# Diagonal score groups as ten blocks of sixteen in a gated attention and maxout kernel on one Trainium2 core

## The chip, the cores and the metric

The kernel runs on one core of a Trainium2 chip. The core has a matrix engine (TensorE, PE in the profile, with its weight loads listed as PEld), three engines for elementwise work (VectorE or DVE, ScalarE or ACT, GpSimd or POOL), a queue engine that only issues transfers here (SyncE or SP), and 16 DMA engines. Data are computed in SBUF, a memory of 128 partitions. TensorE writes to PSUM, from which VectorE and ScalarE fetch its results. The engines run side by side, each through its own instructions in order, and semaphores tie them together. The metric is the device time of one execution in microseconds.

## The reference

```python
scores = scale * np.matmul(z, z.transpose(0, 2, 1))   # z: 8 x 3072 x 64, scale = 1/3072
attn = np.maximum(scores, 0.0) ** 2
x = (u * np.matmul(attn, v)).reshape(24576, 256)      # u, v: 8 x 3072 x 256
h1, h2 = x @ w1, x @ w2                               # w1, w2: 256 x 1024
out = np.maximum(h1, h2) @ w_out                      # w_out: 1024 x 256
```

The scores of a sequence are a product of z with itself, so the matrix of 3072 by 3072 scores is symmetric. There is no softmax: ReLU and square act on each element.

## The kernel before

**Tiling.** A sequence (there are eight) is 24 blocks of 128 rows. Four blocks make a group (`G = 4`), so there are six groups and six steps per sequence, 48 steps in all. Step `n` with group `s` produces the output rows of group `s`; it needs the 512 columns of scores of that group against all six groups of keys. Because the scores are symmetric, a group of scores above the diagonal is computed once and turned by a DMA transpose for the step that needs its mirror image (`add_pair`, job `turn`, tiles `a_sb` to `aT`). The first three steps of the first sequence work without turned tiles.

**The diagonal group** of a step is 4 by 4 blocks of 128 by 128, itself symmetric. `add_diag` (L384) does it in 45 of the 48 steps. Before the change it computes 12 of the 16 blocks: rows 0 and 1 in full, as two matmuls of 512 columns into a PSUM tile of two banks (`scores`), and the lower right quarter of rows 2 and 3 as matmuls of 256 columns into another tile (`scores_low`). The upper right quarter, four blocks, is turned into the lower left one by one DMA transpose within `a_sb` (`do_turn`). The group is stored in `a_sb` as four quarters one behind the other; `blocks` (L488) names the quarters `R(k, t)` for the readers.

**Pairs and the shared tile.** 44 of the 45 diagonal groups come in pairs of neighbouring steps (`st.pair` is 0 or 1; step 3 is alone). A pair shares one PSUM tile, key -1, for its lower right quarters: bank 0 holds those of the first group, bank 1 those of the second. A ReLU (`relu_low`) and a square of half the width of the other ones belong to each group's part.

**Half rows.** A score has 64 terms, so `score` (L209) takes partitions 0 to 63 for one matmul and 64 to 127 for the next (`half`), and the two use the two halves of the array, each into a PSUM bank of its own.

**Sums and products.** Each group of 2 by 2 half-groups is multiplied with v by a scheme of seven products instead of eight. VectorE forms the sums S1 to S4 of quarters (`add_sums`; for diagonal groups S1 is written in place over `R(1, 1)`), and TensorE does the products in two passes: `X` with three products, straight from the quarters, and `Y` with four, from the sums. Behind that come the multiplication with u and the two dense layers (`add_second`: jobs `d`, `g`, `o`, `oc`), three steps late. The second dense layer uses max(h1, h2) = max(h1 - h2, 0) + h2.

**PSUM.** Score tiles, tiles of the dense layers and the shared tiles take turns on three PSUM buffers (`mm_psum`), in the order in which TensorE fills them. A tile can be begun when the one three places ahead of it has been read out.

**The order of work.** The order of TensorE's jobs is written out: the products of all steps in a row (`work`), with visits of up to three score tiles (`windows`) put between them so many nanoseconds ahead of their readers (`laid`). A paired diagonal visit is the three tiles `(n, None)`, `(n, -1)` and `(n + 1, None)` (L1018). For all other engines a planner runs at build time: each job has a cost per engine (`RELU`, `SQUARE`, `TT` and their half-width forms, `PE` costs, SP's cost of a turn), a lag until its result can be used, and a due time that follows from TensorE's plan. The planner simulates the engines with these numbers, picks the next job of each, and decides for ReLUs, squares and copies whether ScalarE or VectorE does them (`left_to_act`, L1374). The program is issued in that order. Turns and stores are issued by SP, loads of u, v, z and weights by POOL.

Of the kernel before, what the change touches and what calls it, by code (L numbers as in the profile page):

```python
# [11 lines left out]
def kernel(  # L12
# [27 lines left out]
    P = 128  # L40
    NSB = S // P
    G = 4
    WIN = 3
    GW = G * P
# [34 lines left out]
    def matmul(*args, **kw):  # L79
        newest[0] = pin(nc.tensor.matmul(*args, **kw)).ins  # L80

    def sp_dma(**kw):
        pin(nc.sync.dma_start(**kw))
# [57 lines left out]
    q = seqs[0]  # L141
# [33 lines left out]
    def job(key, ways, fn, deps=(), new=None, uses=(), after=(), lag=100):  # L175
        assert key not in jobs, key
        jobs[key] = Job(key, ways, fn, deps, new, uses, after, lag)

    def buf(pool, key, make):
        bufs[pool, key] = Buf(make)  # L180
        order.setdefault(pool, []).append(key)

    def tile_of(pool, key):
        return bufs[pool, key].tile
# [24 lines left out]
    def score(q, out_ps, j, k, s, q0, n):  # L209
        half = ds(j * dqk, dqk)  # L210
        matmul(
            out_ps,
            q.zT[half, k + 1 - j, :],
            q.zT[half, ds(G * s + 1 - j + q0, n), :],
            start=True,
            stop=True,
        )

    def turn(out_ap, in_ap):
        sp_dma(out=out_ap, in_=in_ap, transpose=True)  # L220

    def relu(eng, out_ap, in_ap):
        if eng == "ACT":
            pin(nc.scalar.activation(out_ap, in_ap, AF.Relu))  # L224
        else:
            pin(nc.vector.tensor_single_scalar(out=out_ap, in_=in_ap, scalar=0.0, op=ALU.max))  # L226

    def square(eng, ap):
        if eng == "ACT":
            pin(nc.scalar.activation(ap, ap, AF.Square))  # L230
        else:
            pin(nc.vector.tensor_mul(ap, ap, ap))  # L232
# [20 lines left out]
    PE256, PE512, SWITCH = 109, 216, 100  # L253
    TT = {256: 205, 512: 336, 1024: 603}
    RELU = {"ACT": 912, "DVE": 1140}
    RELU_HALF = {"ACT": 480, "DVE": 610}
    SQUARE = {"ACT": 955, "DVE": 603}
    SQUARE_HALF = {"ACT": 530, "DVE": 336}
    COPY_O = {"ACT": 470, "DVE": 610}
    PATIENCE = 200  # L260
    TURN, TURN_LAG, UT_LAG = 1750, 4000, 7000
# [2 lines left out]
    def a_key(n, g):  # L264
        return ("T", ("held", n, g)) if n < HELD and g > 3 else ("A", (n, g))

    def a_tile(st, g):
        return tile_of(*a_key(st.n, g))
# [52 lines left out]
    def s_tile(key):  # L321
        return tile_of("mm", key)
# [4 lines left out]
    def add_pair(st, k0, head=None):  # L327
# [33 lines left out]
        if g > st.s and not direct(st.b, st.s, g):  # L361
# [19 lines left out]
                lag=TURN_LAG + (5000 if st.plain else 0),  # L381
            )

    def add_diag(st):  # L384
        n, q, g = st.n, st.q, st.s
        k = G * g
        a = ("A", (n, g))
        buf("A", (n, g), lambda: apool.tile([P, G, GW], bf16, name="a_sb"))

        def halves():
            return a_tile(st, g).rearrange("p r c -> p (r c)").rearrange("p (h r c) -> p h r c", h=2, r=G)

        def low_blocks():
            return halves()[:, 1, 2:4, :]

        def scores(_):
            for j in range(2):
                score(q, s_tile((n, None))[:, j, :], j, k + j, g, 0, G)  # L400

        low = ("mm", (n - (st.pair or 0), -1))

        def scores_low(_):

            ps = tile_of(*low)
            for r in range(2):
                if st.pair is None:
                    score(q, ps[:, r, : 2 * P], r, k + 2 + r, g, 2, 2)
                else:  # L410
                    for i in range(2):
                        score(q, ps[:, i, ts(r, 2 * P)], i, k + G * i + 2 + r, g + i, 2, 2)

        job(("score", n, None), {"PE": 223}, scores, deps=z_deps(st), new=("mm", (n, None)), lag=150)
        if st.pair != 1:
            job(
                ("score", n, -1),
                {"PE": 112 if st.pair is None else 223},
                scores_low,
                deps=z_deps(st),  # L420
                new=low,
                lag=150,
            )

        def relu_low(eng):
            ps = tile_of(*low)
            if st.pair is None:
                relu(eng, low_blocks(), ps[:, :, : 2 * P])
            else:
                relu(eng, low_blocks(), ps[:, st.pair, :].rearrange("p (r c) -> p r c", r=2))  # L430

        job(
            ("relu", n, None),
            RELU,
            lambda eng: relu(
                eng, halves()[:, :, 0:2, :], s_tile((n, None)).rearrange("p r (h c) -> p h r c", h=2)
            ),
            deps=[("score", n, None)],
            new=a,
            uses=[("mm", (n, None)), a],  # L440
            lag=200,
        )
        job(
            ("relu", n, -1),
            RELU_HALF,
            relu_low,
            deps=[("score",) + low[1]],
            uses=[low, a],
            after=[("relu", n, None)],
            lag=200,  # L450
        )
        job(
            ("square", n, None),
            SQUARE,
            lambda eng: square(eng, halves()[:, :, 0:2, :]),
            deps=[("relu", n, None)],
            uses=[a],
            lag=200,
        )
        job(  # L460
            ("square", n, -1),
            SQUARE_HALF,
            lambda eng: square(eng, low_blocks()),
            deps=[("relu", n, -1)],
            uses=[a],
            lag=200,
        )
        def do_turn(_):
            turn(
                halves()[:, 0, 2:4, :].rearrange("p r (q x) -> p (r q) x", x=P),  # L470
                halves()[:, 1, 0:2, :].rearrange("p r c -> p (r c)"),
            )

        job(
            ("turn", n, None),
            {"SP": 900},
            do_turn,
            deps=[("square", n, None)],
            uses=[a],
            lag=4500,  # L480
        )


# [4 lines left out]
    def blocks(st, g, k, t):  # L488
        if g in st.early:
            turned = tile_of("T", (st.b, g, st.s))  # L490
            return turned.rearrange("p (t j) (k m) x -> p t k j m x", t=2, k=2)[:, t, k]
        if st.diag and g == st.s:
            part = a_tile(st, g).rearrange("p r c -> p (r c)")[:, ts(2 * t + k, GW)]
            form = "p (j m x) -> p m j x" if (k, t) == (1, 0) else "p (m j x) -> p m j x"
            return part.rearrange(form, j=2, m=2)
        return a_tile(st, g).rearrange("p (k m) (t x) -> p k t m x", k=2, t=2)[:, k, t]

    def sums(st, g, f):
# [514 lines left out]
    windows, room = [], 0  # L1013
    for i, (n, k0) in enumerate(tiles):
        if k0 is None and steps[n].pair == 1:
            continue
        if k0 == -1 and steps[n].pair == 0:
            windows.insert(len(windows) - (room > 0), [(n, None), (n, -1), (n + 1, None)])  # L1018
        elif k0 is not None or steps[n].pair is None:
            if not room or (k0 is None and room < 2):  # L1020
                windows.append([])
                room = 2 if n == 0 else WIN
            windows[-1].append((n, k0))
            room -= 1
        if tiles[i + 1 : i + 2] and tiles[i + 1][0] // NG > n // NG:
            room = 0

    begins, t = [], 0
# [19 lines left out]
    for n in range(PLAIN, len(steps)):  # L1048
        i = first_of[n]
# [13 lines left out]
    for w in reversed(range(len(windows))):  # L1063
        limit = min([limit] + [due[r] for r in windows[w] if r in due])
        found = [i for i in spots if begins[i] <= limit]
        i = found[-1] if found else 0
# [26 lines left out]
    def at_step(b, s, us):  # L1093
        return pe_job_at(starts[NG * b + s] + us * 1000)

    def z_deps(st):
        return [("zT", st.b)] if st.b else []
# [45 lines left out]
    for n in range(len(steps)):  # L1143
        b, s = steps[n].b, steps[n].s
        if n == 0:
            add_u(0, None)
        else:
            pb, ps = divmod(n - 1, NG)
# [15 lines left out]
    for tile_sb, source, key, at, new, rows in (  # L1164
# [20 lines left out]
        lag=3500,  # L1185
# [10 lines left out]
    def w2o_products(_):  # L1196
# [18 lines left out]
        lag=150,  # L1215
    )
    for dc in range(KD):
# [6 lines left out]
            lag=200,  # L1224
# [6 lines left out]
    for args in plain_todo:  # L1231
        st, i, ks, dcs = args
# [28 lines left out]
    def held(key):  # L1261
        return a_key(key[1], key[2] // G)[0] == "T"

    slots = sorted(
        [
            (position[at_step(0, key[1] + 2, 1)[0]] if held(key) else position.get(key, -1), k)
            for key, k in turned_order
        ]
        + [(position.get(key, -1), ("held", key[1], k[2])) for key, k in turned_order if held(key)]
        + [(position[at_step(0, 0, 7)[0]], "w2"), (position[at_step(0, 1, 7)[0]], "w2T")],  # L1270
        key=lambda x: x[0],
    )
# [18 lines left out]
    for pool, keys in order.items():  # L1291
        for i, k in enumerate(keys):
            j = taker.get((pool, k))
# [20 lines left out]
    plan, t = {}, 0  # L1314
    for key, before in zip(pe_order, [None] + pe_order):
        j = jobs[key]
# [4 lines left out]
    count = {j.key: len(j.succ) for j in jobs.values()}  # L1321
    stack = [j for j in jobs.values() if not j.succ]
    seen = 0
    while stack:
        j = stack.pop()
# [53 lines left out]
    while len(emitted) < len(jobs) - len(HEAD):  # L1379
        best = None  # L1380
        for e, todo in ready.items():
# [5 lines left out]
            at, _, j = min(found, key=lambda x: x[:2])  # L1387

            late_ones = [x for x in found if x[0] <= at + PATIENCE and x[1] < min(at, j.due)]
            if e != "PE" and late_ones:  # L1390
                at, _, j = min(late_ones, key=lambda x: x[1])
# [3 lines left out]
        at, e, j = best  # L1395
# [93 lines left out]
```

## Time and profile before

| what | value |
|---|---|
| median of three runs | 926.64 us (926.61 to 926.68) |
| the profiled execution's own time | 926.78 us |
| its span | 925.0 us |
| granted TensorE clock | 1.0 of full |
| VectorE busy | 786.2 us, 85% |
| ScalarE busy | 658.3 us, 71% |
| share of q1 (transposes, stores) and q0 (loads) of the 16 DMA engines | 66.9% and 22.6% |
| score matmuls of 512 and of 256 columns | 594 and 90 |
| turns within `a_sb`, and from `a_sb` to `aT` | 45 and 230 |

How to read the profile: the page gives the busy time of each engine, the span in 40 slices, and the chain of work that ended last, followed back from the end. A group of instructions has its line, engine and operation, what it writes and reads (`s_ps<-zT`), the sizes, the number of instructions, then busy time, the mean length of one, and idle time ahead. All matmuls are issued by one helper and so have line 80; they are told apart by their tiles. The timeline lists instructions in order of time, and merges equal ones that follow each other (x8 is eight of them, with the length from the first's start to the last's end); where shapes differ, the first one's is shown. Matmuls are pipelined: a matmul of 512 columns has a recorded length of 379 ns, but the next one starts 216 ns later. So starts are compared, not lengths.

### The profile page before, as it was taken

To read this page: it belongs to the slowest core of one execution; us is meant where nothing else is said; L and a number is where in the kernel's file an instruction comes from. 1 tells how busy PE (TensorE), PEld (TensorE's weight loads), DVE (VectorE), ACT (ScalarE), POOL (GpSimd) and SP (SyncE) were. 2 spreads that over 40 slices of the span, in tenths; PEclk is the share of its full clock that TensorE was granted. 3 is DMA by queue.
4 is the path that set the end of the run, shared out by engine and by line. 5 is a ranking of instruction groups with operands and counts; after the bars stand their busy time and mean duration, and the time that the engine had idled before them with its cause. 6 is when DMAs were issued, how large, how long until landed. Compare 5 with 4: busy or idle time off the path is not lost.

```text
span 925.0 us, 18991 instructions
## 1 busy us (share of the span) xinstructions
PE 918.9 (99%) x7339; PEld 669.8 (72%) x7343; DVE 786.2 (85%) x1955; ACT 658.3 (71%) x785; POOL 58.4 (6%) x115
## 2 busy tenths in 40 slices
PE   8999999999999999999999999999999999999998
PEld 3367777777767776787767877778777786777786
DVE  7948999788998889988899888998789977999661
ACT  8867968758686677856788477884878839787334
POOL 2100100000000000000000010001000010000000
PEclk9999999999999999999999999999999999999999
DMA  9999999988999989999999879999899997997611
GB/s 157 163 197 180 179 184 166 156 152 142 175 169 144 155 145 183 153 148 151 152 185 165 148 131 176 167 164 150 150 151 178 158 168 129 175 151 137 127 35 69
DMA packets 371339, 142.55 MB, mean 154 GB/s; under 512 B 349744, under 2 KB 351408, under 8 KB 371248
## 3 DMA queue, kind: packets, MB, share of 16 engines
q1 hardware_dynamic: 354688, 111.59, 66.9%
q0 software_dynamic: 16560, 29.74, 22.6%
q8 instruction: 57, 0.93, 0.4%
q14 instruction: 34, 0.28, 0.1%
HBM read 59.77 MB, written 25.17 MB: 92 GB/s over the span
## 4 chain that ended last, share of the span: by engine, by line
PE 99%; DMA 0%; ACT 0%; issue 0%; DVE 0%
PE s_ps L80 50%; PE acc L80 49%; DMA o_sb<-in_z_dram 0%; ACT a_sb L230 0%; ACT a_sb L224 0%; PE tpz L109 0%; DVE zT L110 0%; ACT o_sb L235 0%; DVE z_sb L154 0%
## 5 line engine op out<-in xcount | busy, mean ns | idle before, releaser
L80 PEld LDWEIGHTS <-v_sb 128*128 128x128 bf16 x2304 | 224.0, 98 | 79.5 <-issue 37.4
L224 ACT ACTIVATE a_sb<-s_ps 128x1024 bf16<-128x1024 f32 x211 | 204.1, 1019 | 42.3 <-PE s_ps L80 40.8
L80 PE MATMUL acc<-es,v_sb 128*128 128x256 bf16 x864 | 195.8, 274 | 0.0
L80 PE MATMUL s_ps<-w_out_sb,g_sb 128*128 128x256 bf16 x1504 | 194.9, 273 | 0.0
L230 ACT ACTIVATE a_sb<-a_sb 128x1024 bf16<-128x1024 bf16 (+1 forms) x201 | 192.4, 999 | 0.1
L224 ACT ACTIVATE g_sb<-s_ps 128x1024 bf16<-128x1024 f32 x188 | 177.3, 1030 | 11.0 <-PE s_ps L80 10.9
L80 PEld LDWEIGHTS <-lf 128*128 128x128 bf16 x1620 | 158.5, 98 | 22.2
L80 PE MATMUL s_ps<-xT,w_sb 128*128 128x512 bf16 x768 | 173.4, 379 | 0.0
L80 PE MATMUL acc<-es,lf 128*128 128x256 bf16 x756 | 170.8, 273 | 0.0
L80 PE MATMUL acc<-a_sb,lf 128*128 128x256 bf16 x612 | 166.9, 273 | 0.0
L80 PEld LDWEIGHTS <-g_sb 128*128 128x128 bf16 x1504 | 147.1, 98 | 17.3
L80 PE MATMUL acc<-aT,v_sb 128*128 128x256 bf16 x684 | 146.7, 273 | 0.0
L80 PE MATMUL acc<-a_sb,v_sb 128*128 128x256 bf16 (+1 forms) x737 | 143.3, 291 | 0.6 <-issue 0.3
L238 DVE TENSOR_TENSOR es<-a_sb 128x512 bf16<-128x512 bf16 x306 | 122.3, 416 | 25.3 <-PE acc L80 25.0
L235 ACT COPY e<-acc 128x512 f32<-128x512 f32 x90 | 53.0, 589 | 114.9 <-PE acc L80 114.9
L80 PEld LDWEIGHTS <-w_sb 128*128 128x128 bf16 x768 | 75.1, 98 | 80.8
L226 DVE TENSOR_SCALAR a_sb<-s_ps 128x1024 bf16<-128x1024 f32 (+1 forms) x127 | 129.9, 1032 | 1.3 <-PE s_ps L80 0.7
L235 ACT COPY o_sb<-s_ps 128x512 f32<-128x512 f32 (+1 forms) x84 | 48.3, 575 | 91.1 <-PE s_ps L80 91.0
L238 DVE TENSOR_TENSOR es<-aT 128x512 bf16<-128x512 bf16 x126 | 51.2, 418 | 48.0 <-PE acc L80 48.0
L80 PE MATMUL s_ps<-zT 64*128 64x512 bf16 (+1 forms) x684 | 89.7, 366 | 0.3 <-DVE zT L110 0.3
L232 DVE TENSOR_TENSOR a_sb<-a_sb 128x1024 bf16<-128x1024 bf16 (+1 forms) x137 | 86.6, 653 | 0.1
L80 PE MATMUL s_ps<-W2o_sb,xT 128*128 128x256 bf16 x384 | 73.3, 273 | 0.0
(59 smaller groups left out, 726.4 us busy)
## 6 DMA issues: line engine op xcount, KB each, us to landing
out_dram<-o_sb SPq DMA_DIRECT2D x47, 512.0 KB, 4.1
v_sb<-in_v_dram POOLq DMA_DIRECT2D x48, 256.0 KB, 5.2
u_sb<-in_u_dram POOLq DMA_DIRECT2D x48, 256.0 KB, 5.5
aT<-a_sb SPq DMA_TRANSPOSE x230, 4.5
z_sb<-in_z_dram POOLq DMA_DIRECT2D x7, 384.0 KB, 6.2
w_sb<-in_moe_w_dram POOLq DMA_DIRECT2D x2, 512.0 KB, 6.7
uT<-u_sb SPq DMA_TRANSPOSE x48, 4.3
a_sb<-a_sb SPq DMA_TRANSPOSE x45, 2.6
```

The lines of the kernel that those rows point to most:

```text
L80: newest[0] = pin(nc.tensor.matmul(*args, **kw)).ins
L224: pin(nc.scalar.activation(out_ap, in_ap, AF.Relu))
L226: pin(nc.vector.tensor_single_scalar(out=out_ap, in_=in_ap, scalar=0.0, op=ALU.max))
L230: pin(nc.scalar.activation(ap, ap, AF.Square))
L232: pin(nc.vector.tensor_mul(ap, ap, ap))
L235: pin(nc.scalar.copy(out_ap, in_ap) if eng == "ACT" else nc.vector.tensor_copy(out_ap, in_ap))
L238: pin(nc.vector.tensor_add(*args))
```

## The change

A diagonal group is computed as ten of its sixteen blocks, and `a_sb` holds it as 16 slots of one block each.

- The group's own PSUM tile holds eight blocks: (0,0), (0,1), (0,2), (0,3), (2,2), (2,3), (1,2) and (1,3), by four matmuls of 256 columns (two on each half of the array) instead of two of 512. The ReLU puts them into slots 0 to 7 in an order that has the six blocks above the diagonal in slots 2 to 7.
- The shared tile holds the remaining two blocks of each group, (1,1) and (3,3): four matmuls of 128 columns for a pair instead of four of 256, and a ReLU and a square of 256 elements instead of 512 for each group. They go to slots 14 and 15.
- The DMA turns six blocks, slots 2 to 7 into slots 8 to 13, instead of four.
- Readers find a quarter by a first slot, a row step and a column step (`DIAG_SLOTS`, `diag_blocks`) instead of as a contiguous piece.
- The planner's costs follow: 264 and 345 ns for the shared ReLU instead of 480 and 610, 318 and 205 for its square instead of 530 and 336, 60 ns of TensorE for one group's last blocks, 1300 for SP's turn instead of 900, 4700 for its lag instead of 4500.
- In a paired visit the shared tile is the last of the three instead of the middle one.

```diff
-    RELU_HALF = {"ACT": 480, "DVE": 610}
+    RELU_LAST = {"ACT": 264, "DVE": 345}
-    SQUARE_HALF = {"ACT": 530, "DVE": 336}
+    SQUARE_LAST = {"ACT": 318, "DVE": 205}
+    LAST_BLOCKS = 60
...
+    DIAG_SLOTS = {(0, 0): (0, 10, 4), (0, 1): (2, 1, 4), (1, 0): (8, 4, 1), (1, 1): (1, 10, 4)}
+
+    def diag_slots(a):
+        return a.rearrange("p r (s x) -> p (r s) x", x=P)
+
+    def diag_blocks(a, first, row, col):
+        start = diag_slots(a)[:, first, :]
+        return bass.AP(
+            tensor=start.tensor,
+            offset=start.offset,
+            ap=[list(start.ap[0]), [row * P, 2], [col * P, 2], [1, P]],
+        )
...
         def scores(_):
-            for j in range(2):
-                score(q, s_tile((n, None))[:, j, :], j, k + j, g, 0, G)
+            for i in range(2):
+                for j, (row, col) in enumerate(((0, 0), (0, 2)) if i == 0 else ((2, 2), (1, 2))):
+                    score(q, s_tile((n, None))[:, j, ts(i, 2 * P)], j, k + row, g, col, 2)
...
             for r in range(2):
+                row = 2 * r + 1
                 if st.pair is None:
-                    score(q, ps[:, r, : 2 * P], r, k + 2 + r, g, 2, 2)
+                    score(q, ps[:, r, :P], r, k + row, g, row, 1)
                 else:
                     for i in range(2):
-                        score(q, ps[:, i, ts(r, 2 * P)], i, k + G * i + 2 + r, g + i, 2, 2)
+                        score(q, ps[:, i, ts(r, P)], i, k + G * i + row, g + i, row, 1)
...
-                {"PE": 112 if st.pair is None else 223},
+                {"PE": LAST_BLOCKS if st.pair is None else 2 * LAST_BLOCKS},
...
-                relu(eng, low_blocks(), ps[:, :, : 2 * P])
+                relu(eng, slots(14, 2), ps[:, :, :P])
             else:
-                relu(eng, low_blocks(), ps[:, st.pair, :].rearrange("p (r c) -> p r c", r=2))
+                relu(eng, slots(14, 2), ps[:, st.pair, : 2 * P].rearrange("p (r x) -> p r x", r=2))
...
-                eng, halves()[:, :, 0:2, :], s_tile((n, None)).rearrange("p r (h c) -> p h r c", h=2)
+                eng,
+                slots(0, 8).rearrange("p (j r) x -> p j r x", j=2),
+                s_tile((n, None)).rearrange("p h (r j x) -> p j (h r) x", r=2, j=2),
...
-            lambda eng: square(eng, halves()[:, :, 0:2, :]),
+            lambda eng: square(eng, slots(0, 8)),
...
-            lambda eng: square(eng, low_blocks()),
+            lambda eng: square(eng, slots(14, 2)),
...
-            turn(
-                halves()[:, 0, 2:4, :].rearrange("p r (q x) -> p (r q) x", x=P),
-                halves()[:, 1, 0:2, :].rearrange("p r c -> p (r c)"),
-            )
+            turn(slots(8, 6), slots(2, 6).rearrange("p s x -> p (s x)"))
...
-            {"SP": 900},
+            {"SP": 1300},
...
-            lag=4500,
+            lag=4700,
...
-            part = a_tile(st, g).rearrange("p r c -> p (r c)")[:, ts(2 * t + k, GW)]
-            form = "p (j m x) -> p m j x" if (k, t) == (1, 0) else "p (m j x) -> p m j x"
-            return part.rearrange(form, j=2, m=2)
+            return diag_blocks(a_tile(st, g), *DIAG_SLOTS[k, t])
...
-            windows.insert(len(windows) - (room > 0), [(n, None), (n, -1), (n + 1, None)])
+            windows.insert(len(windows) - (room > 0), [(n, None), (n + 1, None), (n, -1)])
```

More of the change, by code (lines that the diff above doesn't have):

```diff
@@ L388, in add_diag, with slots @@
         buf("A", (n, g), lambda: apool.tile([P, G, GW], bf16, name="a_sb"))
[L392 to L396, printed above, removed]
+        def slots(first, count):
+            return diag_slots(a_tile(st, g))[:, ds(first, count), :]
         def scores(_):
-            for j in range(2):
-                score(q, s_tile((n, None))[:, j, :], j, k + j, g, 0, G)
+            for i in range(2):
+                for j, (row, col) in enumerate(((0, 0), (0, 2)) if i == 0 else ((2, 2), (1, 2))):
+                    score(q, s_tile((n, None))[:, j, ts(i, 2 * P)], j, k + row, g, col, 2)
         low = ("mm", (n - (st.pair or 0), -1))
@@ L444, in add_diag @@
             ("relu", n, -1),
-            RELU_HALF,
+            RELU_LAST,
             relu_low,
@@ L461, in add_diag @@
             ("square", n, -1),
-            SQUARE_HALF,
-            lambda eng: square(eng, low_blocks()),
+            SQUARE_LAST,
+            lambda eng: square(eng, slots(14, 2)),
             deps=[("relu", n, -1)],
```

## The prediction, made before the change was measured

> **What bounds the kernel now.** I read the first part of the page, then the chain that ended last, the waits of TensorE, and last the timeline of TensorE around the visits that the change rewrites.
>
> ```profile
> span 925.0 us, 18991 instructions
> PE 918.9 (99%) x7339; PEld 669.8 (72%) x7343; DVE 786.2 (85%) x1955; ACT 658.3 (71%) x785; POOL 58.4 (6%) x115
> ...
> PEclk9999999999999999999999999999999999999999
> ...
> PE 99%; DMA 0%; ACT 0%; issue 0%; DVE 0%
> ```
>
> A busy TensorE is not one at its peak, so the 99% alone proves little. The chain says more: 99% of the way to the end is TensorE following itself. The waits of TensorE from 10 us on are a single line, half a microsecond in three places (shorter waits, in which the array is still finishing its matmul, show only in the pitch further down).
>
> ```profile
> PE acc L80 <- issue: 0.5, 3, 0.2
> ```
>
> The pitch from one start to the next says how densely it runs. Columns of the timeline: start, length, engine, line, operation.
>
> ```profile
> 179.68 2.54 PE L80 MATMUL s_ps<-xT,w_sb 128*128 128x512 bf16 x11
> 187.29 1.04 PE L80 MATMUL s_ps<-w_out_sb,g_sb 128*128 128x256 bf16 x8
> 6.23 1.07 PE L109 MATMUL tpz_c<-ident,z_sb 128*128 128x128 bf16 x16 [0.15 <-DMA z_sb<-in_z_dram]
> ```
>
> With the length of the last one taken off (379, 273 and 220 ns) and divided by the steps, a matmul of 512 columns costs 216 ns, of 256 columns 110 ns, of 128 columns 57 ns, each with weights of its own. The score matmuls read 64 partitions and come in twos, one on each half of the array; the visits show what a pair costs:
>
> ```profile
> 71.70 0.61 PE L80 MATMUL s_ps<-zT 64*128 64x512 bf16 x4
> 72.24 0.28 PE L80 MATMUL acc<-es,v_sb 128*128 128x256 bf16 x1
> ...
> 90.23 0.82 PE L80 MATMUL s_ps<-zT 64*128 64x512 bf16 x6
> 90.99 0.28 PE L80 MATMUL acc<-es,v_sb 128*128 128x256 bf16 x1
> ...
> 137.52 0.82 PE L80 MATMUL s_ps<-zT 64*128 64x512 bf16 x8
> 138.28 0.28 PE L80 MATMUL acc<-a_sb,v_sb 128*128 128x256 bf16 x1
> ...
> 200.01 0.92 PE L80 MATMUL s_ps<-zT 64*128 64x512 bf16 x8
> 200.86 0.28 PE L80 MATMUL acc<-es,v_sb 128*128 128x256 bf16 x1
> ```
>
> Four matmuls of 512 columns take 0.54 us to the next instruction, six take 0.76: a pair costs 0.22, so both halves run at once, and 0.10 us goes to leaving the visit. The third visit is one of the 22 for a pair of diagonal groups: two pairs of 512 and two of 256 columns, again 0.76, so a 256 pair costs 0.11. Its eight matmuls load eight weights and the visit at 90.23 six, in the same time: loads are hidden. The last one took 0.85: its third tile waited 0.08 us for its PSUM buffer, and 0.01 came behind.
>
> So the end moves by what TensorE has to stream, and by waits at visits; everything else has cover.
>
> **The change part by part.** Three prices: pairs at 216, 110 and 57 ns.
>
> Scores. A paired visit now has two pairs of 512 and two of 256: 2×216 + 2×110 = 652 ns. After, each group's tile is two pairs of 256 and the shared tile two pairs of 128: 4×110 + 2×57 = 554 ns. That is 98 ns less, 22 times, 2.16 us. The one unpaired group (step 3) goes from 216 + 110 to 2×110 + 57: 49 ns. Together −2.2 us on the path. The 128 pair on half rows is in no row; its bounds are 57 ns (the 128-column row, one matmul with its load) and 110 ns (it cannot cost more than the wider pair, which also loads twice). At 110 a visit takes 660 and the gain is gone (+0.2 us). I take 57: a 256 pair already costs no more than one 256 matmul, so the pair is nearest to the row of equal columns. 180 more matmul and load instructions come with 90 wider ones split; issue shows no cost, since the second of a pair is 3 to 4 ns behind the first.
>
> ReLU and square of the shared blocks, half as wide.
>
> ```profile
> L226 DVE TENSOR_SCALAR a_sb<-s_ps 128x512 bf16<-128x512 f32 x44 | 28.9, 683 | 0.0
> ...
> L230 ACT ACTIVATE a_sb<-a_sb 128x512 bf16<-128x512 bf16 x30 | 19.0, 633 | 0.0
> ...
> L232 DVE TENSOR_TENSOR a_sb<-a_sb 128x512 bf16<-128x512 bf16 x15 | 6.2, 415 | 0.0
> ...
> a_sb<-a_sb SPq DMA_TRANSPOSE x45, 2.6
> ```
>
> Against the 1024-wide rows (1217, 1063, 682) an element costs 1.04, 0.84 and 0.52 ns, so 256 elements come to 416, 418 and 281 ns. VectorE loses 44×267 + 15×134 = 13.8 us, ScalarE 30×215 = 6.5 us. On the path: nothing, as TensorE hides both. The bound below is what they can give back: 35 visits wait for a ReLU to free the third tile (7 by 0.09, 28 by 0.03 us), 1.5 us in all. I take 0, since those waits are for the 1030 ns ReLUs of the dense layer on ScalarE, which this leaves as they are. The big ReLU, square and sums read the same numbers of elements in runs of 128; diagonal sums already read such runs in one operand at 419 ns against 417, so nothing.
>
> The turn: six blocks for four. Four land in 2.6 us, eight in 4.5 (the rows of a_sb and aT), so six in about 3.6, +1.0. SP's issue of one is 1217 ns for four and 1285 for eight, so +34 ns each, 1.5 us over the span on a queue that only turns and stores follow. Cover: from the landing to the first product that reads it the timeline leaves 5.1 us in step 3, 6.5 in step 4, 12 and more elsewhere. 90 more blocks of 32 KB are 2.9 MB on 111.6 of q1, or 1.8 points of DMA share on 90; tightest there are the v loads, 1.9 us ahead of their first fold. Without the cover the full 1.0 us would come 45 times.
>
> A wait is added: S2 of a diagonal group reads the lower right quarter, which now holds a turned block, so VectorE waits for the turn one sum earlier, with the whole in-order queue behind it. Its start is 6.6 us or more behind the landing; 1.0 later still leaves 5.6. The products waited for the turn before, by their third operand.
>
> The move: the shared tile's scores pass the second group's four matmuls, on TensorE alone. The second group's ReLU can start 0.22 us earlier, the shared ones 0.22 later; ScalarE and VectorE have the 0.22 in the 6.6 us above. The third tile of the visit starts as far in as before (652−216 against 4×110), on the same rotating buffer, so the 0.09 and 0.03 us waits stay.
>
> Sum: 926.78 us is the time of the profiled execution (span 925.0 and 1.8 around it), less 2.2 is 924.6; that run lies 0.14 above the median of 926.64, so against the median 924.4, or 0.24% less. About 0.2%, 1.85 us here, is what a measurement tells from no change, so the forecast lies only 0.4 us beyond it.
>
> **Rivals.** *Narrow pairs don't hide their loads.* If a pair's load begins when the pair before begins to stream and holds for its 94 ns (mean of the 64x128 loads), the 128 pair costs 97 instead of 57: 80 ns of a visit's 98 are lost, the gain is 0.4 us, 926.2. For it: no half-row pair this short is in the trace. Against: the 128-column row keeps 57 ns with loads that last 98.
>
> The Trainium skill (TensorE: Matmul & The Clock Gate, Back-to-back issue gap) gives about 81 ns for a sustained stream of load and matmul at 128 columns. By it a visit saves 50 ns and the time is about 925.5; the row of 57 ns disagrees with it here, for full-height weights.
>
> *Loads on the same rows are never hidden*, so that two more pairs in a visit cost two loads of 94 ns: 188 − 98 = +90 ns, 22 times, +2.0 us: 928.6. The 0.76 us of both visits above speaks against it, as two more loads cost nothing there.
>
> The Trainium skill (same page, Part 3) says that a weight load overlaps matmuls in flight only where the row group differs, which is this rival. The trace disagrees, by the same 0.76.
>
> *A ReLU changes engines* (slower). The planner gives a ReLU to whichever engine ends it first by its own clock, and VectorE gets 13.8 us lighter, ScalarE 6.5. Where the ReLU that frees a third tile goes to VectorE it lasts 1223 instead of 1030 ns, and the wait grows by 193 ns; at all 35 waiting visits 6.8 us: 931.2. It decides from 118 ns at each (4.1 us). For it: the 3 buffers leave no slack there. Against: 191 of 192 of these ReLUs run on ScalarE now, and VectorE remains the fuller one (83% against 70).
>
> *The freed time is worth something*: the 1.5 us of waits go too, 922.9.
>
> *Interleaved slots taken as overlapping*: S1 writes the lower right quarter in place, whose slots now lie between those that the X products read. Were they kept apart, the products that began before S1 ended (7 of the 37 diagonal ones issued behind it) would wait up to 0.42 us each, 2.9 in all: 927.3. Against: off the diagonal the regions interleave already, and there S1 began before products issued ahead of it had ended 36 times of 170.
>
> **How the numbers follow.** Forecast 0.58 (own range 923.9 to 925.1, 0.04 of it above the bound), loads not hidden at 128 columns 0.10, never hidden 0.03, ReLU on VectorE 0.14 (0.04 of it too small to tell), waits gone 0.10, interleaved slots 0.05. Faster: 0.54 + 0.10 = 0.64. Same: 0.04 + 0.10 + 0.04 + 0.05 = 0.23. Slower: 0.10 + 0.03 = 0.13. The range 922.8 to 926.8 leaves out most of the ReLU case, the never hidden loads and part of the slots, about 0.2.
>
> **What would show it.** Score rows of 64x256 x180, 64x128 x90, 64x512 x504; a paired visit of 0.66 us without a wait; VectorE about 772 us busy, ScalarE about 652; turns of a_sb landing in about 3.6; no wait of TensorE named for a turn or a sum. Wrong would be a paired visit of 0.76 (narrow pairs), third tiles that wait longer or in more visits (ReLU), or products of a diagonal group waiting on VectorE (slots).

## The result, and the profile after

The changed kernel takes 924.58 us against 926.84 us for the kernel before (medians of 22 runs each), a ratio of 0.9979 with a 95% interval of 0.9972 to 0.9985. That is 2.26 us less; the forecast was 2.2 less. The interval runs from 0.15% to 0.28%, so the gain is clear of zero; that it lies beyond 0.2%, as forecast, holds for the median and not for the whole interval. One run of the kernel before, beside the second set of experiments, took 1922.7 us and is left out of the ratios.

The page of the changed kernel, the lines that answer to those of before:

```profile
span 924.1 us, 19122 instructions
PE 917.6 (99%) x7429; PEld 673.3 (73%) x7433; DVE 771.0 (83%) x1911; ACT 653.3 (71%) x829; POOL 58.4 (6%) x115
...
PEclk9999999999999999999999999999999999999999
...
PE 95%; DMA 1%; issue 1%; DVE 1%; ACT 0%; POOL 0%; POOLq 0%
```

TensorE is still nearly the whole chain. The 1% each of DMA and VectorE is one event in this one execution, which took 925.82 us, more than the median: a load of v came late (section "The late load of v"); the changed kernel's second profile (span 922.9 us) has no such wait.

The visits, from the timeline of TensorE, in the same columns as before:

```profile
251.69 0.72 PE L80 MATMUL s_ps<-zT 64*128 64x256 bf16 x12
252.34 0.28 PE L80 MATMUL acc<-a_sb,v_sb 128*128 128x256 bf16 x1
...
278.35 0.75 PE L80 MATMUL s_ps<-zT 64*128 64x256 bf16 x12
279.03 0.28 PE L80 MATMUL acc<-es,v_sb 128*128 128x256 bf16 x1
...
313.98 0.81 PE L80 MATMUL s_ps<-zT 64*128 64x256 bf16 x12
314.72 0.28 PE L80 MATMUL acc<-es,v_sb 128*128 128x256 bf16 x1
```

There are three kinds of paired visits, and each kind comes at the same place in every sequence. From the first score to the next instruction they take 0.65, 0.68 and 0.74 us. Before they took 0.76 (the one at 137.52), 0.79 (164.28) and 0.85 (200.01): without a wait, with a wait of about 0.03 for the third tile's buffer, and with one of about 0.09. The one at 164.28, in the kernel before:

```profile
164.28 0.86 PE L80 MATMUL s_ps<-zT 64*128 64x512 bf16 x8
165.07 0.28 PE L80 MATMUL acc<-es,v_sb 128*128 128x256 bf16 x1
```

Each is 0.10 to 0.11 shorter, and the waits are still there. By the starts of the single matmuls, before against the second profile of the changed kernel, the difference is 102 ns in each of the seven visits without a wait, 104 in each of the 15 with one, and 52 in the unpaired one: 7 × 102 + 15 × 104 + 52 = 2.33 us, the whole gain.

The groups by form show what became of the shared blocks:

```profile
L80 PE MATMUL s_ps<-zT 64*128 64x512 bf16 x504 | 70.8, 382 | 0.2 <-DVE zT L110 0.2
...
L230 ACT ACTIVATE a_sb<-a_sb 128x256 bf16<-128x256 bf16 x38 | 16.2, 425 | 0.0
L224 ACT ACTIVATE a_sb<-s_ps 128x256 bf16<-128x256 f32 x44 | 14.4, 384 | 0.0
L80 PE MATMUL s_ps<-zT 64*128 64x256 bf16 x180 | 13.8, 272 | 0.0
...
L80 PE MATMUL s_ps<-zT 64*128 64x128 bf16 x90 | 6.5, 217 | 0.0
```

The counts are the expected ones. But 44 of the 45 shared ReLUs now run on ScalarE, where 44 ran on VectorE before. The planner's new costs are not the reason: with the old costs (`e3_old_costs`, first line) the same 44 are on ScalarE, and also in the kernel before with nothing changed but the order within a visit (`e8_move_only`, second line). So the later place of the shared tile sends them there.

```profile
L224 ACT ACTIVATE a_sb<-s_ps 128x256 bf16<-128x256 f32 x44 | 14.4, 385 | 0.0
...
L224 ACT ACTIVATE a_sb<-s_ps 128x512 bf16<-128x512 f32 x44 | 23.8, 597 | 0.0
```

### The profile page after: what moved, and what is told of

Same layout as the page of the kernel before. It is cut to its first block, busy times and chain, and to the rows that moved or that the text cites. A ratio compares the mean times of both kernels' runs of the same rounds, so it can differ in the third digit from the quotient of the medians.

```text
span 924.1 us, 19122 instructions
## 1 busy us (share of the span) xinstructions
PE 917.6 (99%) x7429; PEld 673.3 (73%) x7433; DVE 771.0 (83%) x1911; ACT 653.3 (71%) x829; POOL 58.4 (6%) x115
## 3 DMA queue, kind: packets, MB, share of 16 engines
q1 hardware_dynamic: 366208, 114.54, 70.6%
## 4 chain that ended last, share of the span: by engine, by line
PE 95%; DMA 1%; issue 1%; DVE 1%; ACT 0%; POOL 0%; POOLq 0%
PE s_ps L80 48%; PE acc L80 47%; DMA v_sb<-in_v_dram 1%; DVE es L238 0%; DMA o_sb<-in_z_dram 0%; DVE lf L241 0%; POOL v_sb L87 0%; DVE a_sb L226 0%; ACT a_sb L230 0%; DVE a_sb L238 0%; ACT a_sb L224 0%; DVE v_sb L241 0%; PE tpz L109 0%; POOL u_sb L87 0%; DVE zT L110 0%
## 5 line engine op out<-in xcount | busy, mean ns | idle before, releaser
L224 ACT ACTIVATE a_sb<-s_ps 128x1024 bf16<-128x1024 f32 (+1 forms) x231 | 194.9, 903 | 40.5 <-PE s_ps L80 39.8
L226 DVE TENSOR_SCALAR a_sb<-s_ps 128x1024 bf16<-128x1024 f32 x107 | 129.3, 1210 | 5.8 <-PE s_ps L80 5.2
L235 ACT COPY o_sb<-s_ps 128x512 f32<-128x512 f32 (+1 forms) x98 | 56.6, 578 | 97.2 <-PE s_ps L80 97.2
L80 PE MATMUL s_ps<-zT 64*128 64x512 bf16 (+2 forms) x774 | 87.8, 337 | 0.2 <-DVE zT L110 0.2
L232 DVE TENSOR_TENSOR a_sb<-a_sb 128x1024 bf16<-128x1024 bf16 (+1 forms) x127 | 80.9, 660 | 0.0
```

What stands on the lines that cost most here:

```text
L235: pin(nc.scalar.copy(out_ap, in_ap) if eng == "ACT" else nc.vector.tensor_copy(out_ap, in_ap))
```

## Experiments

### What TensorE streams: last blocks scored wide again

```diff
-                    score(q, ps[:, r, :P], r, k + row, g, row, 1)
+                    score(q, ps[:, r, : 2 * P], r, k + row, g, row - 1, 2)
...
-                        score(q, ps[:, i, ts(r, P)], i, k + G * i + row, g + i, row, 1)
+                        score(q, ps[:, i, ts(r, 2 * P)], i, k + G * i + row, g + i, row - 1, 2)
```

The ReLU reads the right half of each 256 columns.

> The two last blocks of each group are scored with their left neighbour as before the change, so the shared tile is again four matmuls of 256 columns; its ReLU reads only the last blocks, and all else is as in the changed kernel. Streaming theory: every paired visit is longer by 2 x 53 ns, 22 times, and the time goes back by 2.3 us to 926.6 (ratio to the kernel before 1.000). Rival (the gain comes from the lighter VectorE and ScalarE, which stay light here): 924.4, ratio 0.9977.

It took 927.06 us, ratio 0.9999 (0.9990 to 1.0008). The changed kernel, beside it on the same chip, was expected as follows:

> The changed kernel once more, as the yardstick beside the experiments of this set. Streaming theory (the gain is TensorE's shorter visits, 22 x 102 ns): a run in which no transfer is late takes 924.2 to 924.6 us, 2.3 less than before. Late-transfer theory (the larger turns make loads of v late around the second sequence in some executions): now and then 1 to 3 us more, with a wait of VectorE for v in the profile; without that cause all runs lie within 0.4 us.

It took 924.69 us, ratio 0.9978 (0.9970 to 0.9987). A visit without a wait is 0.76 us again in the wide version:

```profile
251.63 0.83 PE L80 MATMUL s_ps<-zT 64*128 64x256 bf16 x12
252.39 0.28 PE L80 MATMUL acc<-a_sb,v_sb 128*128 128x256 bf16 x1
```

VectorE (772.6 us) and ScalarE (654.6) stay as light there as in the changed kernel, and the gain is gone. So it is the streamed columns, and the lighter work of the two other engines is worth nothing by itself.

### The order within a visit: two orders, wide and narrow

The changed kernel with the shared tile in the middle, as before the change:

```diff
-            windows.insert(len(windows) - (room > 0), [(n, None), (n + 1, None), (n, -1)])
+            windows.insert(len(windows) - (room > 0), [(n, None), (n, -1), (n + 1, None)])
```

> The changed kernel with the shared tile back in the middle of its visit. Streaming theory: the visits stream the same columns in another order, so the time stays at 924.2 to 924.6 in runs without a late load of v. Rival (the move itself gives part of the gain, by freeing PSUM buffers in a better order): 0.5 us or more above the changed kernel, with a longer wait of the third tile or of the tile after the visit.

It took 926.88 us, ratio 0.9999 (0.9990 to 1.0008): the streaming theory, as I had put it, missed. The same columns in another order lose nearly all. The timeline, first a visit without a wait, then one of the longest:

```profile
252.47 0.72 PE L80 MATMUL s_ps<-zT 64*128 64x256 bf16 x12
253.13 0.28 PE L80 MATMUL acc<-a_sb,v_sb 128*128 128x256 bf16 x1
...
314.91 0.92 PE L80 MATMUL s_ps<-zT 64*128 64x256 bf16 x12
315.76 0.28 PE L80 MATMUL acc<-es,v_sb 128*128 128x256 bf16 x1
```

The visit without a wait keeps the gain (0.66 us), the one with a wait is back at 0.85, as before the change. The third tile's buffer comes free when ScalarE's ReLU of a dense tile ends, a moment that scores do not move. In the kernel before, ahead of the long visit at 200.01, these are the two ReLUs:

```profile
198.54 1.95 ACT L224 ACTIVATE g_sb<-s_ps 128x1024 bf16<-128x1024 f32 x2
```

They end at 200.49, and the third tile's first matmul starts at 200.54. With the narrow tile in the middle the third tile is reached 106 ns earlier and waits 106 ns longer, and then streams its two 256 pairs as ever. In a visit that waits, the end is the release plus the columns of the last tile, and only what stands last counts. Fifteen of the 22 paired visits wait; at 107 ns each they cost 1.6 us, and seven ordinary visits behind a dense stage take 46 ns more (0.3 us): 1.9 us of the 2.3. The 0.4 us that is left is too little for these medians to show.

To see whether the move pays without the narrow blocks, the kernel before with that line changed the other way:

> The kernel before with only the order within a paired visit changed: the shared tile, still four matmuls of 256 columns, comes last. Theory from the two orders of the changed kernel (a visit that waits ends at the release of its third tile's buffer plus the columns of that tile, so the move pays only where the last tile is narrow): both last tiles stream 216 ns here, so 0, ratio 1.000. Rival (the move pays by itself): 924.5 to 925.5, ratio 0.998 to 0.999.

It took 926.96 us, ratio 1.0001 (0.9992 to 1.0010). Its longest visits stay at 0.85:

```profile
313.47 0.92 PE L80 MATMUL s_ps<-zT 64*128 64x512 bf16 x8
314.32 0.28 PE L80 MATMUL acc<-es,v_sb 128*128 128x256 bf16 x1
```

So by the visits the move alone gives nothing, the narrow blocks alone some 0.4 us (too little for the medians to tell), and both give 2.3: the move lets the 15 waiting visits keep what the narrow blocks save.

### Are weight loads hidden on rows that are streaming?

The kernel before with its diagonal score matmuls of 512 columns split in two:

```diff
-            for j in range(2):
-                score(q, s_tile((n, None))[:, j, :], j, k + j, g, 0, G)
+            for i in range(2):
+                for j in range(2):
+                    score(q, s_tile((n, None))[:, j, ts(i, 2 * P)], j, k + j, g, 2 * i, 2)
```

> The kernel before, with each 512-column score matmul of a diagonal group split into two of 256: the same columns, four more weight loads and two more pairs per paired visit. Hidden loads: ratio to the kernel before 1.000, a paired visit still 0.76 us to the next instruction. Rival (a load on rows that are streaming is never hidden): two more pairs with a 94 ns load each, 22 times, +4.1 us, ratio 1.0045.

It took 926.88 us, ratio 1.0001 (0.9993 to 1.0010). A visit without a wait still takes 0.76 us:

```profile
253.61 0.83 PE L80 MATMUL s_ps<-zT 64*128 64x256 bf16 x12
254.37 0.28 PE L80 MATMUL acc<-a_sb,v_sb 128*128 128x256 bf16 x1
```

By the starts of the matmuls, from the last product ahead of the visit to the first behind it, it goes from 960 to 965 ns. Two more pairs with four more loads cost 5 ns, not 188. The Trainium skill (TensorE: Matmul & The Clock Gate, Part 3) has a load overlap only where the row group differs. This run does not bear that out: here the loads of a pair start within 15 ns of the start of the pair before it, which streams through both halves for another 90 ns and more.

### Does the plan decide?

The planner's costs back to 480 and 610, 530 and 336, 112, 900 and 4500:

> The planner's costs for the shared ReLU and square, the last scores and the turn are put back to the values of before, so VectorE's and ScalarE's jobs are assigned and ordered by old prices; the instructions are those of the changed kernel. Streaming theory: the gain does not hang on the plan, 924.3 to 924.8. Rival (a ReLU that changes engines decides): over 926, with longer waits of the third tile.

It took 924.59 us, ratio 0.9974 (0.9966 to 0.9983). The gain does not hang on the new costs. What they do move is smaller: 14 output copies and 8 of the shared squares go from VectorE to ScalarE in the changed kernel and not in this version.

### How much cover is there in the other direction?

Each shared ReLU done twice (`for _ in range(2):` ahead of both calls in `relu_low`):

> Each shared ReLU of the changed kernel is done twice over the same data, which changes nothing in the result and gives VectorE and ScalarE back more than the change took from that ReLU (about 45 x 0.35 = 16 us). Cover theory (work of these engines is hidden): 924.4 to 925.0 in runs without a late load. Rival (their lighter load is where the gain came from): back to 926 or more.

It took 930.66 us, ratio 1.0038 (1.0026 to 1.0050), 6 us over the changed kernel, though TensorE has the same work. My cover theory missed. The largest wait of TensorE in its profile, and the ordinary visit at 258 us, which takes 0.79 us (257.62 to 258.41) in the changed kernel's second profile:

```profile
PE s_ps L80 <- ACT g_sb L224: 3.3, 14, 0.3
...
258.62 0.61 PE L80 MATMUL s_ps<-zT 64*128 64x512 bf16 x4
259.53 0.39 PE L80 MATMUL s_ps<-zT 64*128 64x512 bf16 x2 [0.31 <-ACT g_sb L224]
259.85 0.28 PE L80 MATMUL acc<-es,v_sb 128*128 128x256 bf16 x1
```

The 88 shared ReLUs are on ScalarE (381 ns each), so a second one puts it behind, and behind the paired visit without a wait comes a dense stage whose four ReLUs then start late. TensorE waits 0.3 us for a dense tile's buffer and 0.45 more at the next visit, in each sequence. By the shift between the two traces that is 0.86 us in each of seven sequences, 6.0 us.

The same with the planner told of it (528 and 690):

> The doubled shared ReLU again, with its cost doubled in the planner (528 and 690 ns). The doubling alone cost 6 us over the changed kernel. Theory A (the loss came from a plan that did not know of the work): the planner moves other jobs and most of it goes, 924.4 to 926. Theory B (ScalarE has no room at the one place in each sequence where it was lost, whatever the plan): 929 to 931.

It took 928.53 us, ratio 1.0025 (1.0016 to 1.0034), between the two theories; six of its runs lie at 927.8 to 928.5, five at 929.3 to 931.5. A plan that knows of the work gets back 2 of the 6 us. What its profile still loses to the changed kernel's second one (span 926.2 against 922.9 us) is 0.48 us at that same visit in each of seven sequences, so ScalarE has no room ahead of that stage under this plan either:

```profile
PE s_ps L80 <- ACT g_sb L224: 2.4, 7, 0.3
```

### The late load of v

In the profiled execution of the changed kernel, the fold of the second sequence's last group waited:

```profile
119.76 0.29 DVE L241 TENSOR_TENSOR lf<-v_sb 128x256 bf16<-128x256 bf16 x1 [2.38 <-DMA v_sb<-in_v_dram]
...
130.48 0.27 PE L80 MATMUL acc<-es,v_sb 128*128 128x256 bf16 x1 [0.70 <-DVE es L238]
```

That load landed 11.0 us after its issue, against 5.2 in the profile of before, and VectorE with its sums behind it passed the delay on to TensorE. Since the turn is the one thing that the change makes larger on the DMA queues, I suspected it:

```diff
-    DIAG_SLOTS = {(0, 0): (0, 10, 4), (0, 1): (2, 1, 4), (1, 0): (8, 4, 1), (1, 1): (1, 10, 4)}
+    DIAG_SLOTS = {(0, 0): (0, 10, 4), (0, 1): (2, 1, 4), (1, 0): (2, 1, 4), (1, 1): (1, 10, 4)}
...
-            turn(slots(8, 6), slots(2, 6).rearrange("p s x -> p (s x)"))
+            turn(slots(8, 4), slots(2, 4).rearrange("p s x -> p (s x)"))
```

This version leaves the lower left quarter unturned, so it does not compute the reference's output; only its time is of use.

> The turn moves four blocks of each group instead of six, as before the change; the lower left quarter is read from the slots of the upper right one, so the two blocks left out are never turned. All else as in the changed kernel. Late-transfer theory: the occasional 1 to 3 us go, all runs lie at 924.1 to 924.5, and the wait of VectorE for v in the second sequence is gone. Rival (the new order of jobs makes those waits): spread and wait stay as in the changed kernel.

It did not come out so. The times lie in two clusters, four runs at 924.29 to 924.57 and seven at 925.9 to 926.9 (median 926.13), and its profile has the wait again:

```profile
DVE lf L241 <- DMA v_sb<-in_v_dram: 2.8, 1, 2.8
```

On the same chip the changed kernel had two of 11 runs above 926, and the kernel before nine of 33 above 928; a profile of the kernel before with split matmuls, whose turns are the old ones, has a wait for v too. So smaller turns do not remove it. Five of the 13 profiles have this wait at the same fold, of 2.0 to 2.8 us: the changed kernel's first one, four turned, old costs, split before, and visits later. In the first two of these the turns are one behind at 60 us (14 issued against 15 in the second profile of the changed kernel), but so they are in profiles without the wait; what makes some executions late is open. Nor is every long execution of this kind: the profile of the shared tile in the middle (928.05 us) has no such wait, and TensorE is there 1.4 us behind the changed kernel's second profile already at 15 us.

Planning the folds later was meant to make VectorE immune to it (lag of a load of v 12000 instead of 8000):

> The changed kernel with a longer lag in the planner for loads of v, 12000 ns instead of 8000, so the folds that read v are planned later on VectorE; no instruction is added. Late-load theory (the runs of 926 and more are those in which VectorE sits at a fold with the sums of the next products behind it): the fast runs stay at 924.2 to 924.6 and the slow ones shrink by about 1 us or go; no wait for v is left in the profile. Rival (the late transfers reach TensorE by another way, a turn or u): the spread stays.

It took 940.59 us (four runs), ratio 1.0146 (1.0131 to 1.0161). The folds were then too late for their products:

```profile
PE acc L80 <- DVE lf L241: 13.2, 7, 2.2
```

That is 1.9 us in each of seven places, paid in every execution against a delay that is there in some.

### A version that beats both

The waits that remain at visits were left as a given by the prediction. All 36 visits that wait start 872 ns of planned work behind a dense stage, and here they are put one product job later:

```diff
+    later = {}
+    for i in sorted(laid):
+        behind = begins[i] - max([end for _, end in shared if end <= begins[i]], default=0)
+        later.setdefault(i + 1 if 860 <= behind < 900 and not work[i + 1][1] else i, []).extend(laid[i])
+    laid = later
```

> The changed kernel with each of the 36 visits that start 872 ns of planned work behind a dense stage put one product job (436 ns) later, so that their third tile's buffer is free when it is reached. Theory (the waits of 0.03 and 0.09 us and the 0.01 to 0.02 behind each are all that is lost there): 36 waits, 1.6 us, go, and runs without a late load take 922.6 to 923.0. Rival (the next visit then comes 436 ns too soon for its own buffers): new waits at later visits, no gain or a loss.

It took 923.50 us, ratio 0.9964 (0.9952 to 0.9977), about 1.1 us below the changed kernel. The visit that had waited longest no longer waits:

```profile
314.19 0.72 PE L80 MATMUL s_ps<-zT 64*128 64x256 bf16 x12
314.84 0.28 PE L80 MATMUL acc<-es,v_sb 128*128 128x256 bf16 x1
```

All 22 paired visits take the same 0.65 us now, and against the changed kernel's second trace 0.23 us go in each sequence, 1.6 in all, as expected. The median shows 1.1 of them; this kernel has only five runs, of 923.1 to 924.5, and its profiled one (924.47) has the late load, so the rest of the difference is not located.

## Why the prediction was right, point by point

**The bound and the sum.** TensorE's own stream set the end, and the sum of −2.2 us came out as 2.26 by the medians and 2.33 by the pitches (102 to 104 ns a visit where 98 were worked out, 52 for 49). The step that carried most doubt was the price of a 128-column pair on half rows, with bounds of 57 and 110 ns. It is 56 ns: the second of a pair starts 3 ns behind the first and the next pair 53 ns later. The two rivals about loads fall, one by that number, the other by the split visits. The figure of about 81 ns that the Trainium skill (TensorE: Matmul & The Clock Gate, Back-to-back issue gap) gives for a stream of 128 columns is not met by it either.

**The move.** The prediction priced it at nothing, since the third tile is reached as far into the visit as before. That sum (652−216 against 440 ns) is right and is just what makes the change work: the alternative order would have reached it 106 ns sooner and lost 1.9 us. So "on TensorE alone" was too little said of this step. It did not see that in a waiting visit only the last tile's columns count, and that the forecast of 22 equal gains hung on the move. Adding up all columns gave the right number for the 15 waiting visits because the narrow tile stands last; that part was luck. Nor did it see that the later place of the shared tile makes the planner send 44 shared ReLUs to another engine.

**The waits.** The 0.03 and 0.09 us stayed, as forecast. There are 29 of the short ones, not 28, so 36 visits in all and 1.6 us.

**ReLU and square.** "On the path: nothing" is right for what was taken away (wide last blocks: light engines, no gain). The split was wrong: the working kept each job on its engine, 13.8 us off VectorE and 6.5 off ScalarE. Measured are 15.2 and 5.0, but with other jobs: the planner sent 44 shared ReLUs, 14 output copies and 8 shared squares from VectorE to ScalarE and 23 full-width ReLUs the other way, so that the totals lie so near is luck. That ReLUs change engines is the rival's mechanism, at jobs where it did no harm; but the move set it off, not the lighter work. The sentence on cover was also one-sided: doing each shared ReLU twice adds 4 to 6 us to the changed kernel.

**The turn.** Six blocks land in 3.0 us by the median, not 3.6; four take 2.6. The share of q1 on the DMA engines rose by 3.7 points in the profiled execution and by 1.4 in the second (66.9 to 70.6 and 68.3), around the 1.8 worked out. No wait of TensorE is named for a turn. The prediction named the loads of v as the tightest cover, and they are what moved the profiled execution; but they come late without the change too, as the profile of the split version shows.

**S2's wait and the interleaved slots.** The second profile of the changed kernel names no wait of VectorE for a transfer other than the opening's z, and none of TensorE for a sum. Both stayed at nothing.

## What to carry to other kernels

When one engine's own stream is the chain, count its columns at the pitch that the trace shows and ask, at each place where it also waits, which piece stands behind the wait: time saved ahead of a wait is given back there, time saved behind it is kept. So put the shortest piece last in a stage that ends on a release, and better still move the stage until the wait is gone, which here was worth another 1.1 us. An engine that is 71% busy can still have no room at one place per round; that it may lose work for nothing does not mean that it can take more.

## What the runs showed of the hardware that was not expected

Two matmuls on the two halves of the array with weights of their own can follow each other every 56 ns at 128 columns (53 plus 3), with all four weight loads of two pairs hidden, and splitting two 512 pairs into four 256 ones costs 5 ns. A wait leaves a trail: a third tile that waits 16 to 19 ns for its buffer makes the visit 29 to 34 ns longer, since its second matmul follows 6 instead of 3 ns behind and what comes next is another 10 to 13 ns late. The same 256 KB load of v, issued at 108.8 us, took 11.0 us to land in one profile of the changed kernel and 4.6 in the other.
